# Transposing W_spatial as pairs of bf16 values in fp32 words

## The chip, the cores and the metric

The kernel runs on one core of one Trainium2 chip. The metric is the device time of one execution in microseconds, as the median of several runs; the kernel before was run three times: 140.18, 140.47 and 141.69 us. A core has five engines that run side by side, each with its own queue of instructions: TensorE (PE in the profile, with PEld for its weight loads), VectorE (DVE), ScalarE (ACT), GpSimd (POOL) and SyncE (SP, which here only issues transfers). PE writes its results to PSUM, eight banks of 512 fp32 words on each of 128 partitions. DVE and ACT copy from there to SBUF.

## What is computed

Two layers follow each other. The first is a linear attention with decay (4 batches, 8 heads, 768 positions, head size 64), worked out in blocks. Its output, 768 rows of 512 values for each batch, is the input x of the second, a gated MLP:

```python
h = np.maximum(x @ w_in, 0.0)
u, v = (h[..., :d_ff // 2].copy(), h[..., d_ff // 2:].copy())
mu = np.mean(v, axis=-1, keepdims=True)
var = np.mean((v - mu) ** 2, axis=-1, keepdims=True)
v_n = (v - mu) / np.sqrt(var + 1e-06)
v_s = np.einsum('ts,bsd->btd', w_spatial, v_n) + b_spatial[None, :, None]
gated = u * v_s
return (gated @ w_out).astype(np.float32)
```

`w_spatial` is 768 x 768 (t x s) in fp32. The sum over s is a matmul on PE, which sums over the partitions, so s must lie on the partitions: the kernel needs W_spatial transposed, and makes it itself.

## The kernel before

The work is cut into 12 units n of 256 positions, three for each batch (n // 3 is the batch). For each unit the kernel loads q, k and v, scales q and k by powers of the decay (QM, KM), turns them with transposes on PE (TQ, TK), forms masked scores (SC, MK), the attention output (AV) and from it x, already transposed (EX). Then come the second half of w_in (PV, EV), the statistics and the normalisation of v (BN, RA, RD, VN) and the first half of w_in (PU, EU). When the three units of a batch are done, the spatial matmuls (PW, line 567) and the output (PO, PH) of that batch follow.

The order of the whole is written out by hand: the string ORDER lists some 1,000 tokens. A token such as `EW.1.0.3.D` names a step, its numbers and, at the end, the engine (T for PE, D, A, P, S). Each engine takes its own tokens in that order, and an instruction that has to wait holds up all that stand behind it on its engine. Waits between engines follow from what each step reads and writes.

The steps that the change and the prediction speak of:

- WQ (line 270): six transfers bring the rows of W_spatial, 128 at a time, as fp32 into staging tiles.
- WC (line 273): casts one such chunk of rows to bf16 into `wsp_raw[:, a]` (128 partitions, 768 values). Chunks 0, 1, 3 and 4 are cast on POOL, 2 and 5 on ACT. On POOL the casts of 4 and 3 stand behind GN (line 532), a copy of one element that waits for VN.2.1.
- WT (line 550): transposes. `WT.k.i` takes the two column blocks 2k and 2k + 1 of the three row chunks of half i, six 128 x 128 blocks of bf16, into one bank. There are six WT (k from 0 to 2, i from 0 to 1), 36 transposes, in three places of PE's order: WT.1.0, WT.0.0 and WT.2.0 together, then WT.2.1 and WT.0.1, then WT.1.1.
- EW (line 559): copies the 768 values of a bank (in each partition) to `wt_sb[:, 2k:2k + 2, ...]`. EW.0.0, EW.2.1 and EW.0.1 run on ACT, EW.1.0, EW.2.0 and EW.1.1 on DVE, through the common helper `copy` (lines 178 and 180).
- VN (line 523): writes a normalised chunk of v. On DVE, VN.2.1 and VN.0.1 stand directly behind EW.1.0 and EW.2.0.
- PW (line 565): a spatial matmul for one half i and one block of 128 columns f: six matmuls over the chunks s from 0 to 5, with chunk s of `vn` as weights and `wt_sb[:, s]` as the moving operand. Chunk s of `wt_sb` is written by EW with k = s // 2. VN.0.1 writes chunk 1 of `vn`, VN.2.1 chunk 5.
- BB (line 291): spreads the bias over the partitions with an fp32 matmul of one row. FL (line 304): filling matmuls on ones. Both run in the first microseconds.
- VC (line 348): the cast of v to bf16; VC.0 is the first, on POOL.
- GM (line 571): the product of u with a finished PW on DVE. MK (line 397): the masking of the scores on DVE.

A bank of PSUM is named by the last number of a token. A step that writes a bank waits until the one that reads it last is done.

Of the kernel before, what the change touches and what calls it, by code (L numbers as in the profile page):

```python
# [8 lines left out]
FP32 = mybir.dt.float32  # L9
BF16 = mybir.dt.bfloat16  # L10
# [6 lines left out]
lam.A BR.A tab.0.A LK.0.S LQ.0.S LV.0.S LQ.1.S LK.1.S LK.2.S LV.1.S LQ.2.S WH.0.S posk.P idn.P msk.P one.D row.D  # L17
WH.1.S FL.1.512.1.1.T FL.1.256.0.1.T FL.1.256.3.1.T FL.1.256.3.1.T FL.1.512.3.1.T FL.1.256.1.1.T FL.1.512.6.1.T LB.6.T
FL.1.256.4.1.T FL.1.256.3.1.T BB.1.5.T BB.0.2.T LN.6.A LL.D mkc.D LX.A QM.0.0.P TQ.0.0.1.T KM.0.0.D KM.0.1.D QM.0.1.P
TK.0.0.0.T TK.0.1.4.T EK.0.0.0.D QM.1.0.D QM.1.1.D BE.1.5.A BE.0.2.A EQ.0.0.1.A EK.0.1.4.A VC.0.P SC.0.0.0.1.T  # L20
TQ.0.1.3.T EQ.0.1.3.A KP.0.6.T TQ.1.0.2.T SC.0.1.4.5.T TQ.1.1.3.T KM.1.1.P KM.1.0.P MK.0.0.0.1.D KM.2.1.P KM.2.0.P
VD.1.1.P TK.1.1.0.T EQ.1.0.2.A SX.0.A EK.1.1.0.A VD.1.0.A MK.0.1.4.5.D EQ.1.1.3.D FL.1.256.2.1.T TK.1.0.1.T
SC.1.1.2.3.T eps.D SY.0.6.D EK.1.0.1.D MK.1.1.2.3.D QM.2.1.P CW.0.P CW.1.P AV.0.0.6.1.T SC.1.0.4.5.T TK.2.1.0.T
# [62 lines left out]
def kernel(  # L86
# [12 lines left out]
    nc = tc.nc  # L99
    P = 128  # L100
    B, H, S, D = q.shape
# [9 lines left out]
    HW = S // 2  # L111
    NVH = NT // 2
# [5 lines left out]
    def sb(shape, dt, name):  # L118
        return const.tile(shape, dt, name=name)

    def many(n, shape, dt, name):
        return [const.tile(shape, dt, name=f"{name}_{i}") for i in range(n)]
# [7 lines left out]
    ident = sb([P, P], BF16, "ident")  # L130
    mfull = sb([P, 2, 2, P], BF16, "mfull")
    m01 = sb([P, 2, 2, Q64], BF16, "m01")
    posk = sb([P, NR, 2], FP32, "posk")
# [8 lines left out]
    mv = many(2, [P, NT, 2], FP32, "mv")  # L142
    rstd = many(2, [P, NT], FP32, "rstd")
    gap = sb([P, 120], FP32, "gap")
    win_sb = sb([P, NCH, DFF], BF16, "win_sb")
    wout_sb = sb([P, NCH, DM], BF16, "wout_sb")
    wsp_raw = sb([P, NT, S], BF16, "wsp_raw")
    wt_sb = sb([P, NT, S], BF16, "wt_sb")
# [24 lines left out]
    def bank(b):  # L173
        return ps[:, b]

    def copy(e, o, i):
        if e == "A":
            nc.scalar.activation(out=o, in_=i, func=AF.Copy)  # L178
        elif e == "D":
            nc.vector.tensor_copy(out=o, in_=i)  # L180
        else:
            nc.gpsimd.tensor_copy(out=o, in_=i)
# [43 lines left out]
    def c_ident(e):  # L226
        make_identity(nc, ident)

    def c_mask(e):
        nc.gpsimd.memset(mfull, 1.0)  # L230
        nc.gpsimd.affine_select(out=mfull, in_=mfull, compare_op=ALU.is_ge, fill=0.0, base=0,
                                pattern=[[-1, 2], [1, 2], [2, P]], channel_multiplier=-2)
# [32 lines left out]
    def stage(a):  # L265
        if a // 2 == 1:
            return wss[:, a % 2]
        return wst[a // 4].rearrange("p g f -> p (g f)")[:, (a % 2) * S:(a % 2 + 1) * S]
# [2 lines left out]
        nc.sync.dma_start(out=stage(a), in_=moe_w_spatial[a * P:(a + 1) * P, :])  # L271

    def w_c(e, a):
        copy(e, wsp_raw[:, a], stage(a))

    def w_out(e):
        nc.gpsimd.dma_start(out=wout_sb, in_=moe_w_out.rearrange("(t p) f -> p t f", p=P))
# [270 lines left out]
             bank(b).rearrange("p (f x) -> p f x", f=2))  # L548

    def w_t(e, k, i, b):  # L550
        for h in range(2):
            for a in range(NVH):
                nc.tensor.transpose(out=trip(b)[:, h, a], in_=wsp_raw[:, NVH * i + a, (2 * k + h) * P:(2 * k + h + 1) * P],  # L553
                                    identity=ident)

    def trip(b):
        return bank(b).bitcast(BF16)[:, 0:S].rearrange("p (h a x) -> p h a x", h=2, a=NVH)

    def e_w(e, k, i, b):
        copy(e, wt_sb[:, 2 * k:2 * k + 2, i * HW:(i + 1) * HW], trip(b).rearrange("p h a x -> p h (a x)"))  # L560

    def g_p(e, bb, f, i, b):
        copy(e, bank(b)[:, 0:HW], bsp[:, i * HW:(i + 1) * HW])
# [35 lines left out]
    def st_o(e, bb, t):  # L599
        eng = {"S": nc.sync, "A": nc.scalar}[e]  # L600
        eng.dma_start(out=out[bb, t * P:(t + 1) * P, :], in_=o_sb[(bb * NT + t) % NO])

    ops = dict(GT=after, GN=after_vn, one=c_ones, FL=f_l, FX=f_x, WP=w_p, WX=w_x, FN=f_n, lam=c_lam, posk=c_posk, tab=c_tab, row=c_row, eps=c_eps, LB=l_b, LN=l_n, LL=l_l, LX=l_x, idn=c_ident, msk=c_mask, mkc=c_mask2, WI=w_in, WS=w_sp, WO=w_out, BR=b_r, BB=b_b, BE=b_e, HL=hold, WH=w_h, CW=c_w, CX=c_x, WQ=w_q, WC=w_c,
               LK=ld_k, LQ=ld_q, LV=ld_v, KM=k_m, QM=q_m, DK=d_k, DQ=d_q, VC=v_c, VD=v_d, TK=t_k, TQ=t_q, EK=e_k, EQ=e_q,
               SC=s_c, MK=m_k, KV=k_v, SS=s_s, KP=k_p, SX=s_x, SY=s_y, SA=s_a, BQ=b_q, AV=a_v, EX=e_x, PV=p_v, EV=e_v, BN=b_n, RA=r_a, RD=r_d, RB=r_b,
               VN=v_n, PU=p_u, EU=e_u, WT=w_t, EW=e_w, PW=p_w, GP=g_p, GM=g_m, PO=p_o, EO=e_o, ST=st_o, PH=p_h, EH=e_h, SH=s_h)
    with tc.manual_schedule():
        for token in ORDER.split():
# [32 lines left out]
```

## Time and profile before

| | us |
|---|---|
| runs, median (lowest to highest) | 140.47 (140.18 to 141.69) |
| profiled execution: span of its instructions | 138.7 |
| profiled execution: its own whole time | not recorded; median less span is 1.8 |
| PE busy | 132.4 |
| DVE busy | 111.3 |
| ACT busy | 82.8 |
| POOL busy | 53.2 |
| the 36 transposes of W_spatial, first start to last start | 31.6 to 38.8 |

The span runs from the first to the last instruction of the program. Times in the profile count from its start. A row of a group has the line of the kernel, the engine, the operation, what it writes and reads, how many, then the busy time in us and the mean of one in ns, then the idle time of the engine just before them and what ended it. A row of a timeline has the start and the length in us, the engine, line and operation, and in brackets the idle time before. A row of the chain that ended last has start, length, engine, what is written, line and count: it is the sequence of work that led to the last instruction, followed backwards, each piece either released by the one ahead of it or standing behind it on the same engine. A matmul's own duration (219 ns for a transpose) is longer than the step from one to the next, since matmuls overlap; on the chain the step counts. Weight loads overlap with matmuls too.

### The profile page before, as it was taken

Reading aid. Unit: us, or ns where it says so; the run is one execution under the profiler, and the core shown is the slowest. Engines: PE = TensorE matmul, PEld = TensorE weight load, DVE = VectorE, ACT = ScalarE, POOL = GpSimd, SP = SyncE. Lnnn points to the kernel's source line nnn. Section 1 sums busy time; section 2 is a strip of 40 time slices with the busy share of each in tenths; the row PEclk is TensorE's granted clock in tenths of the full one; section 3 lists DMA queues with packets and bytes.
Section 4 is the critical chain, followed back from the end, with each engine's and each line's share of the span. In section 5 each row is a group of like instructions: output and inputs, shape, how many; then the busy total and the mean of one; then the engine's idle time right before and its main releaser. Section 6 shows DMA issues by size and latency. Waiting matters only on the chain.

```text
span 138.7 us, 4697 instructions
## 1 busy us (share of the span) xinstructions
PE 132.4 (95%) x1980; PEld 85.1 (61%) x1980; DVE 111.3 (80%) x229; ACT 82.8 (60%) x159; POOL 53.2 (38%) x64
## 2 busy tenths in 40 slices
PE   5998799999999999999999999999999999999990
PEld 2556665688667557667566565766655664766550
DVE  1549999989688879999979987887969988887540
ACT  3355579799846655598903678795716553961241
POOL 5178734862979676900068033209500000000000
PEclk9999999999999999999999999999999999999999
DMA  3999999999999999669796799999976594000165
GB/s 78 347 346 347 388 361 359 411 378 356 262 368 335 261 285 337 149 164 354 226 219 145 189 344 277 247 223 349 127 227 65 198 395 181 9 0 0 76 255 199
DMA packets 56873, 34.12 MB, mean 246 GB/s; under 512 B 13843, under 2 KB 52243, under 8 KB 56852
## 3 DMA queue, kind: packets, MB, share of 16 engines
q1 hardware_dynamic: 56704, 33.69, 83.7%
q8 instruction: 15, 0.25, 0.7%
q10 hardware_dynamic: 148, 0.13, 0.3%
q14 instruction: 6, 0.05, 0.1%
HBM read 24.38 MB, written 6.29 MB: 221 GB/s over the span
## 4 chain that ended last, share of the span: by engine, by line
PE 89%; DVE 5%; ACT 2%; issue 2%; DVEq 0%
PE ps L567 23%; PE ps L541 15%; PE ps L578 14%; PE ps L490 12%; PE ps L363 5%; PE ps L393 5%; PE ps L465 4%; DVE a_sb L398 3%; PE ps L456 2%; PE ps L422 2%; PE ps L306 2%; PE ps L292 2%; PE ps L553 1%; PE ps L587 1%; ACT vh L495 1%
## 5 line engine op out<-in xcount | busy, mean ns | idle before, releaser
L567 PE MATMUL ps<-wt_sb,vn 128*128 128x384 bf16 x192 | 32.4, 326 | 0.0
L328 POOL TENSOR_TENSOR kc<-k_in,lv 128x512 bf16<-128x512 f32 x20 | 20.5, 1043 | 30.7 <-DMA k_in<-in_k_dram 15.6
L398 DVE TENSOR_TENSOR a_sb<-ps,m 128x1024 bf16<-128x1024 f32 x24 | 28.7, 1218 | 2.4 <-PE ps L393 1.6
L567 PEld LDWEIGHTS <-vn 128*128 128x128 bf16 x192 | 18.5, 98 | 12.0
L541 PE MATMUL ps<-xT,win_sb 128*128 128x256 bf16 x192 | 23.8, 273 | 0.0
L490 PE MATMUL ps<-win_sb,xT 128*128 128x512 bf16 x96 | 22.7, 379 | 0.0
L578 PE MATMUL ps<-wout_sb,gT 128*128 128x512 bf16 x88 | 21.5, 380 | 0.0
L541 PEld LDWEIGHTS <-win_sb 128*128 128x128 bf16 x192 | 18.3, 98 | 4.5
L573 DVE TENSOR_TENSOR gT<-ps,uT 128x384 bf16<-128x384 f32 x32 | 17.0, 552 | 5.1 <-PE ps L567 5.1
L328 POOL TENSOR_TENSOR qc<-q_in,lqn 128x512 bf16<-128x512 f32 x17 | 17.7, 1059 | 5.0 <-DMA q_in<-in_q_dram 5.0
L505 DVE BATCH_NORM_STATS2 st<-vh 128x6 f32<-128x512 bf16 x24 | 16.3, 678 | 0.9 <-ACT vh L495 0.5
L490 PEld LDWEIGHTS <-xT 128*128 128x128 bf16 x96 | 9.0, 98 | 10.1 <-ACT xT L178 1.0
L178 ACT ACTIVATE xT<-ps 128x512 bf16<-128x512 f32 x21 | 11.5, 593 | 6.0 <-PE ps L465 6.0
L178 ACT ACTIVATE o_sb<-ps 128x512 f32<-128x512 f32 (+1 forms) x17 | 9.4, 555 | 9.3 <-PE ps L578 5.5
L495 ACT ACTIVATE vh<-ps 128x512 bf16<-128x512 f32 x19 | 10.8, 596 | 7.0 <-PE ps L490 6.9
L495 ACT ACTIVATE uT<-ps 128x512 bf16<-128x512 f32 x22 | 12.7, 594 | 3.1 <-PE ps L541 2.8
L178 ACT ACTIVATE ps<-bsp 128x384 f32<-128x384 f32 x22 | 10.5, 496 | 6.4 <-DVE gT L573 3.6
L578 PEld LDWEIGHTS <-gT 128*128 128x128 bf16 x88 | 8.1, 97 | 8.0 <-issue 0.2
L393 PE MATMUL ps<-qT,kT 64*64 64x128 bf16 x384 | 9.9, 226 | 0.6 <-DVE qT L180 0.5
L465 PE MATMUL ps<-a_sb,vb 64*64 64x128 bf16 x384 | 10.2, 217 | 0.2
L180 DVE COPY o_sb<-ps 128x512 f32<-128x512 f32 (+1 forms) x9 | 5.9, 657 | 3.3 <-PE ps L578 3.2
L465 PEld LDWEIGHTS <-vb 64*64 64x64 bf16 x384 | 7.3, 107 | 1.6 <-issue 1.5
(75 smaller groups left out, 164.5 us busy)
## 6 DMA issues: line engine op xcount, KB each, us to landing
k_in<-in_k_dram SPq DMA_DIRECT2D x12, 512.0 KB, 6.5
q_in<-in_q_dram SPq DMA_DIRECT2D x12, 512.0 KB, 6.4
v_in<-in_v_dram SPq DMA_DIRECT2D x12, 512.0 KB, 6.3
out_dram<-o_sb SPq DMA_DIRECT2D x22, 256.0 KB, 2.4
wst<-in_moe_w_in_dram SPq DMA_DIRECT2D x4, 512.0 KB, 7.7
wst<-in_moe_w_spatial_dram SPq DMA_DIRECT2D x4, 384.0 KB, 6.4
wst<-in_moe_w_out_dram SPq DMA_DIRECT2D x1, 1024.0 KB, 7.7
wss<-in_moe_w_spatial_dram SPq DMA_DIRECT2D x2, 384.0 KB, 6.7
```

The costliest lines, as they stand in the source:

```text
L178: nc.scalar.activation(out=o, in_=i, func=AF.Copy)
L328: vec(e).tensor_tensor(out=dst[n % NCA][:, u].rearrange("p u m o d -> p o (u m) d"), in0=src[n % NIN].rearrange("p (o u) m d -> p o u m d" ...
L393: nc.tensor.matmul(out=pa[o][row(c), w, j], lhsT=kT[n % NTR][row(o), u, j, c * Q64:(c + 1) * Q64], rhs=qv(n, o, u, c), start=(w == 0 and j ...
L398: nc.vector.tensor_tensor(out=a_sb[n % NA][:, i].rearrange("p o w j x -> p o w (j x)"), in0=ps[:, b0:b1 + 1:b1 - b0].rearrange("p o (w y) ...
L465: nc.tensor.matmul(out=po[c ^ o][row(w), c, i], lhsT=vb[n % NCA][row(c), 4 * o + u, j, :], rhs=a[row(c), i, o, w, j, :], start=(r == 0 and ...
L490: nc.tensor.matmul(out=bank(b), lhsT=x[:, slot(c, g)], rhs=win_sb[:, g, DH:DFF], start=(g == 0), stop=(g == NCH - 1))
L495: nc.scalar.activation(out=o, in_=i, func=AF.Relu)
L505: nc.vector.bn_stats(out=st6[p2][:, t], in_=vh[p2][:, t])
L541: nc.tensor.matmul(out=pu[:, f2].rearrange("p (c x) -> p c x", c=2), lhsT=win_sb[:, g, f * P:(f + 1) * P], rhs=x[:, slot(0, g):slot(1, g) ...
L567: nc.tensor.matmul(out=bank(b)[:, 0:HW], lhsT=vn[bb % 2][:, s, f * P:(f + 1) * P], rhs=wt_sb[:, s, i * HW:(i + 1) * HW], start=False, stop ...
L573: nc.vector.tensor_tensor(out=gT[bb % 2][:, f, cols], in0=bank(b)[:, 0:HW], in1=uT[bb % 2][:, f, cols], op=ALU.mult)
L578: nc.tensor.matmul(out=bank(b), lhsT=gT[bb % 2][:, f, t * P:(t + 1) * P], rhs=wout_sb[:, f, :], start=(f == 0), stop=(f == NCH - 1))
```

## The change

The cast WC now writes its 768 bf16 values in another order: of the column blocks 2k and 2k + 1, column x of the first and column x of the second become neighbours and so one 4-byte word. WT then reads `wsp_raw` as fp32, 384 words to a row, and transposes 128 x 128 blocks of words against an identity in fp32: three in place of six for each WT, 18 in place of 36 in all. After it a bank holds the words, each with a value of block 2k and one of block 2k + 1, and EW takes them apart when it copies: it reads the 2-byte values at a step of two, first all of one half, then all of the other. The result in `wt_sb` is as before. The fp32 identity is a new tile, filled by one copy on POOL (`idf`), placed in the order behind VC.0. Nothing else of the order changes.

```diff
-... VC.0.P SC.0.0.0.1.T
+... VC.0.P idf.P SC.0.0.0.1.T
...
+    ident4 = sb([P, P], FP32, "ident4")
...
+    def c_ident4(e):
+        nc.gpsimd.tensor_copy(out=ident4, in_=ident)
...
     def w_c(e, a):
-        copy(e, wsp_raw[:, a], stage(a))
+        copy(e, wsp_raw[:, a].rearrange("p (k x h) -> p k h x", h=2, x=P),
+             stage(a).rearrange("p (k h x) -> p k h x", h=2, x=P))
...
     def w_t(e, k, i, b):
-        for h in range(2):
-            for a in range(NVH):
-                nc.tensor.transpose(out=trip(b)[:, h, a], in_=wsp_raw[:, NVH * i + a, (2 * k + h) * P:(2 * k + h + 1) * P],
-                                    identity=ident)
-
-    def trip(b):
-        return bank(b).bitcast(BF16)[:, 0:S].rearrange("p (h a x) -> p h a x", h=2, a=NVH)
+        for a in range(NVH):
+            nc.tensor.transpose(out=bank(b)[:, a * P:(a + 1) * P],
+                                in_=wsp_raw[:, NVH * i + a].bitcast(FP32)[:, k * P:(k + 1) * P], identity=ident4)
 
     def e_w(e, k, i, b):
-        copy(e, wt_sb[:, 2 * k:2 * k + 2, i * HW:(i + 1) * HW], trip(b).rearrange("p h a x -> p h (a x)"))
+        copy(e, wt_sb[:, 2 * k:2 * k + 2, i * HW:(i + 1) * HW],
+             bank(b).bitcast(BF16)[:, 0:S].rearrange("p (y h) -> p h y", h=2))
```

More of the change, by code (lines that the diff above doesn't have):

```diff
@@ L19 @@
 FL.1.256.4.1.T FL.1.256.3.1.T BB.1.5.T BB.0.2.T LN.6.A LL.D mkc.D LX.A QM.0.0.P TQ.0.0.1.T KM.0.0.D KM.0.1.D QM.0.1.P
-TK.0.0.0.T TK.0.1.4.T EK.0.0.0.D QM.1.0.D QM.1.1.D BE.1.5.A BE.0.2.A EQ.0.0.1.A EK.0.1.4.A VC.0.P SC.0.0.0.1.T
+TK.0.0.0.T TK.0.1.4.T EK.0.0.0.D QM.1.0.D QM.1.1.D BE.1.5.A BE.0.2.A EQ.0.0.1.A EK.0.1.4.A VC.0.P idf.P SC.0.0.0.1.T
 TQ.0.1.3.T EQ.0.1.3.A KP.0.6.T TQ.1.0.2.T SC.0.1.4.5.T TQ.1.1.3.T KM.1.1.P KM.1.0.P MK.0.0.0.1.D KM.2.1.P KM.2.0.P
@@ L601, in st_o @@
         eng.dma_start(out=out[bb, t * P:(t + 1) * P, :], in_=o_sb[(bb * NT + t) % NO])
-    ops = dict(GT=after, GN=after_vn, one=c_ones, FL=f_l, FX=f_x, WP=w_p, WX=w_x, FN=f_n, lam=c_lam, posk=c_posk, tab=c_tab, row=c_row, eps=c_eps, LB=l_b, LN=l_n, LL=l_l, LX=l_x, idn=c_ident, msk=c_mask, mkc=c_mask2, WI=w_in, WS=w_sp, WO=w_out, BR=b_r, BB=b_b, BE=b_e, HL=hold, WH=w_h, CW=c_w, CX=c_x, WQ=w_q, WC=w_c,
+    ops = dict(GT=after, GN=after_vn, one=c_ones, FL=f_l, FX=f_x, WP=w_p, WX=w_x, FN=f_n, lam=c_lam, posk=c_posk, tab=c_tab, row=c_row, eps=c_eps, LB=l_b, LN=l_n, LL=l_l, LX=l_x, idn=c_ident, idf=c_ident4, msk=c_mask, mkc=c_mask2, WI=w_in, WS=w_sp, WO=w_out, BR=b_r, BB=b_b, BE=b_e, HL=hold, WH=w_h, CW=c_w, CX=c_x, WQ=w_q, WC=w_c,
                LK=ld_k, LQ=ld_q, LV=ld_v, KM=k_m, QM=q_m, DK=d_k, DQ=d_q, VC=v_c, VD=v_d, TK=t_k, TQ=t_q, EK=e_k, EQ=e_q,
```

## The prediction

> **What bounds the kernel now.** I read the page first, then the chain that ended last in order of time, then the groups by line and shape, then the timelines of single engines around the transposes. The page says which engine sets the end:
>
> ```profile
> span 138.7 us, 4697 instructions
> PE 132.4 (95%) x1980; PEld 85.1 (61%) x1980; DVE 111.3 (80%) x229; ACT 82.8 (60%) x159; POOL 53.2 (38%) x64
> PE 89%; DVE 5%; ACT 2%; issue 2%; DVEq 0%
> ```
>
> TensorE (PE) is busy 95% of the span and holds 89% of the chain, so time added to or taken from PE in the middle moves the end about one for one. The three runs have a median of 140.47 us; the span is 138.7, so 1.8 us lie around it, and I leave these as they are. A measurement of this kernel can tell about 1% (1.4 us) from no change.
>
> All the changed transposes (line 553) lie on the chain:
>
> ```profile
> 31.79 1.00 PE ps L553 x18
> 32.79 0.87 PE ps L541 x8
> 33.66 0.35 PE ps L393 x16
> 34.01 2.06 PE ps L567 x12
> 36.07 0.67 PE ps L553 x12
> 36.74 1.95 PE ps L567 x12
> 38.69 0.34 PE ps L553 x6
> 39.02 0.38 PE ps L422 x32
> 39.40 0.23 PE ps L393 x16
> 39.62 2.06 PE ps L567 x12
> 41.68 0.89 PE ps L363 x16
> ```
>
> The reader is to see three bursts, 18 + 12 + 6, in 1.00 + 0.67 + 0.34 = 2.01 us, 56 ns each, with no wait of PE between them. Call the three places A, B and C. Half of 2.01 us, 1.0, is the most that 18 fewer transposes at the same pace can bring.
>
> **Part 1, the transposes.** 36 leave, 18 come, each still 128 columns, but of 4-byte elements. No fp32 transpose is in the trace. The lower bound is the row of the same operation, 56 ns. The upper bound is the only fp32 matmul on PE, the spreading of the bias:
>
> ```profile
> 1.52 2.31 PE L306 MATMUL ps<-ones 128*128 128x512 bf16 x7 [1.52 <-DVE ones L302]
> 4.83 2.92 PE L292 MATMUL ps<-bsp,one_row 1*128 1x384 f32 x4
> L292 PEld LDWEIGHTS ps<-bsp,one_row x4: 283/332/332, 4.8 to 6.3; 1*128 1x128 f32 x4
> L306 PEld LDWEIGHTS <-ones x10: 98/133/151, 1.5 to 12.7; 128*128 128x128 bf16 x10
> ```
>
> Both stand in the slow first microseconds, so I use their ratio alone. The seven fillers (three of 512 columns, four of 256) stream 2560 columns in 2.31 us, 0.90 ns a column. The two fp32 matmuls became four instructions, 2.92 us for 2 x 384 columns, 3.8 ns a column: 4.2 times as much. Carried over, an fp32 transpose would take 4.2 x 56 = 235 ns. Between the two lies a case where only the weight load doubles (283 to 332 against up to 151 ns in the same microseconds) and sets the pace: 2 x 56 = 112 ns. I take 56 ns, because the transpose of line 553 is the nearest row in operation, shape and place, and the fp32 row multiplies and is split in two instructions. All three prices go on into the range.
>
> The Trainium skill ("TensorE: Matmul & The Clock Gate", Terms) says that on trn2 the matmul and the weight load have a transpose mode that is four times as fast for FP32. By that rule 235 would become 59 ns and the sum below would stay; by the fp32 row alone it would be that of the first rival. No run here shows which.
>
> **Part 2, the copies out of PSUM (EW).** Three run on VectorE (DVE), three on ScalarE (ACT). They now read bf16 values two apart, one from each 4-byte word.
>
> ```profile
> L180 DVE COPY wt_sb<-ps 128x768 bf16<-128x768 bf16 x3 | 1.7, 554 | 0.2
> L180 DVE CAST xT<-ps 128x512 bf16<-128x512 f32 x3 | 2.0, 665 | 0.0
> L180 DVE COPY kT<-ps 128x512 bf16<-128x512 bf16 x3 | 1.2, 416 | 2.0 <-PE ps L363 2.0
> L178 ACT ACTIVATE wt_sb<-ps 128x768 bf16<-128x768 bf16 x3 | 2.3, 809 | 0.8 <-PE ps L553 0.8
> L178 ACT ACTIVATE xT<-ps 128x512 bf16<-128x512 f32 x21 | 11.5, 593 | 6.0 <-PE ps L465 6.0
> L178 ACT ACTIVATE qT<-ps 128x512 bf16<-128x512 bf16 x4 | 2.4, 597 | 1.3 <-PE ps L363 1.2
> ```
>
> On ACT, 512 elements cost 593 ns from 4-byte words and 597 from packed ones: the new read costs it nothing, 809 stays. On DVE they cost 665 from words and 416 packed, 249 more. A strided bf16 read is not in the trace: its bounds are 554 (packed pace) and 554 + 249 x 768/512 = 928 ns (a word for each element). I take 928, as each element now sits in a word of its own, like the fp32 row's. The Trainium skill ("VectorE: DVE Perf Modes", Mode 2×_1P) asks for a step of one for the two-a-cycle mode; by it the copy is 928 and not 554, the side against this change. No run here shows a step of two.
>
> What the 0.37 us more meets at A:
>
> ```profile
> 31.40 0.72 DVE L529 TENSOR_SCALAR vn<-vh,mv,rstd 128x512 bf16<-128x512 bf16 x2
> 32.16 1.23 DVE L180 COPY wt_sb<-ps 128x768 bf16<-128x768 bf16 x2
> 33.30 0.73 DVE L529 TENSOR_SCALAR vn<-vh,mv,rstd 128x512 bf16<-128x512 bf16 x2
> 34.06 1.22 DVE L398 TENSOR_TENSOR a_sb<-ps,m 128x1024 bf16<-128x1024 f32 x1
> 33.94 0.10 PEld L567 LDWEIGHTS <-vn 128*128 128x128 bf16 x1
> 34.09 0.29 PEld L567 LDWEIGHTS <-vn 128*128 128x128 bf16 x3
> ```
>
> DVE is full here. EW.1.0 and EW.2.0 end at 33.39, then VN.2.1 and VN.0.1 end at 34.03, and the second weight load of the first spatial matmul (line 567, chunk s = 1, which is VN.0.1's output) starts at 34.09, 0.06 later. So DVE and PE arrive there together. With the change DVE is free for EW.1.0 at 32.16 as before (its transposes are done), two copies of 0.93 overlapping by 0.08 end at 33.94, the two VN 0.64 later at 34.58, and the load starts at 34.64: **+0.55 us**. PE itself would be there at 33.59, half a microsecond early, and waits about 1.05 us. The 0.50 us that A's nine fewer transposes save is therefore lost, and 0.55 more.
>
> At B the copies are ACT's. PE saves 6 x 56 = **-0.33 us**. What B waits for is the last casts of W_spatial on GpSimd (POOL), behind a marker copy that waits for VN.2.1:
>
> ```profile
> 33.77 0.30 POOL L533 CAST seen<-vn 1x1 f32<-1x1 bf16 x1 [3.45 <-DVE vn L529]
> 34.02 0.82 POOL L182 CAST wsp_raw<-wst 128x768 bf16<-128x768 f32 x1
> 34.79 0.82 POOL L182 CAST wsp_raw<-wss 128x768 bf16<-128x768 f32 x1
> 38.56 2.03 POOL L328 TENSOR_TENSOR kc<-k_in,lv 128x512 bf16<-128x512 f32 x2
> ```
>
> These move with VN by 0.55 and end at 36.16, PE arrives at 36.62: still 0.46 of cover. The four tensor products behind them (up to 40.59) feed transposes of line 363 that start at 41.68 on the chain, over 1 us later, and PE moves too.
>
> At C the copy EW.1.1 is DVE's again:
>
> ```profile
> 38.73 0.56 DVE L573 TENSOR_TENSOR gT<-ps,uT 128x384 bf16<-128x384 f32 x1 [0.35 <-PE ps L567]
> 39.20 0.55 DVE L180 COPY wt_sb<-ps 128x768 bf16<-128x768 bf16 x1
> ```
>
> It starts when the product before it is done and would end at 39.20 + 0.93 = 40.13. The third matmul of the chain's row at 39.62 (chunk s = 2, 0.17 us each) reads it at 39.96. With 0.06 for the hand-over it waits until 40.19: **+0.23 us**; the 0.17 that three fewer transposes save is lost there too.
>
> **Part 3, the casts into pairs (WC) and the fp32 identity.** Four casts on POOL and two on ACT now write every second 2-byte slot. No strided write of one element is in the trace; the packed cast's 0.82 us is the lower bound and twice it (one slot at a time where two were packed) the upper. I take 0.82: it is 1.07 ns an element, and DVE's word-at-a-time row is no faster (665 ns for 512), so nothing says that POOL packs. The new copy of the identity is 128 elements on POOL after VC.0:
>
> ```profile
> 8.61 1.03 POOL L182 CAST vb<-v_in 128x1024 bf16<-128x1024 f32 x1
> 10.88 4.04 POOL L328 TENSOR_TENSOR kc<-k_in,lv 128x512 bf16<-128x512 f32 x4 [1.24 <-DMA k_in<-in_k_dram]
> ```
>
> By the POOL cast above it is at most 0.82 us and falls into 1.24 us of waiting for a load: nothing. Without that cover it would delay the products of the second block by its length.
>
> **Sum.** A +0.55, B -0.33, C +0.23: +0.45 us, 140.47 + 0.45 = 140.9 us. At 112 ns a transpose A and C stay as they are (DVE sets both) and B saves nothing: +0.78, 141.25. I let no later part of the chain take the delay back, since DVE's longest wait is one for PE, which moves with it:
>
> ```profile
> L573 DVE TENSOR_TENSOR gT<-ps,uT 128x384 bf16<-128x384 f32 x32 | 17.0, 552 | 5.1 <-PE ps L567 5.1
> ```
>
> **Rivals.**
>
> *Slower: fp32 transposes at 235 ns.* At A the third ends at 31.79 + 0.71 = 32.50 and the ninth at 33.91; EW.2.0 then runs 33.95 to 34.88, VN.0.1 ends at 35.52, the load starts at 35.58, +1.49. B costs 6 x 235 - 670 = +0.74. At C three end at 39.40, EW.1.1 at 40.37, the reader starts at 40.43, +0.47. Sum +2.7: 143.2 us. For it: the only fp32 row on PE. Against: that row is arithmetic, in two instructions. It decides from about 150 ns on, where the total passes +1.4. Chance 0.18.
>
> *Faster: DVE reads at the packed pace.* EW.1.0 and EW.2.0 no longer wait for the ninth pair of transposes (0.11 us) and overlap (0.08): A -0.20; B -0.33; C, where EW.1.1 still ends at 39.75, -0.15. Sum -0.68: 139.8 us. For it: the values are still 2 bytes. Against: 665 against 416 ns. Chance 0.10.
>
> *POOL's casts take twice as long.* Behind VN.2.1 (33.71 + 0.55) and the marker the two last casts would end at 37.80, PE arrives at 36.62: 1.2 us of wait at B, 142.1 us. Against: 1.07 ns an element leaves no packing to lose. Chance 0.10.
>
> **How the numbers follow.** The forecast with transposes of 56 to 112 ns and DVE's copies at 0.93 has chance 0.57 and its own range 140.5 to 141.6; 0.05 is for what I don't see. The range, 139.7 to 143.1, takes in the faster rival, POOL's, and the larger part of the way to the slow transposes. Slower by over 1% (above 141.9): 0.18, most of POOL's 0.10, and a little, 0.28. Faster by over 1% would need more than the whole 1.0 us: 0.03. Within 1%: 0.69.
>
> **What would show it.** Right: 18 instructions in place of 36 at the transposes' line, 56 ns apart on the chain; DVE's copies into wt_sb at about 0.93 us and ACT's at 0.81; a new idle time of about 1 us of PE before line 567's weight load, ended by DVE's vn, and one of about 0.4 us ended by wt_sb; POOL's casts at 0.82. Wrong: two instructions for a transpose or a pitch above 150 ns; DVE's copies near 0.55; PE waiting at B for wsp_raw; or the delay gone again by the second group of spatial matmuls at 66 us.

## The result and the profile after

The changed kernel takes 142.49 us in the median (142.11 to 142.51 in four runs), the kernel before 140.33 in the runs beside it: ratio 1.0138, 95% interval 1.009 to 1.0186 (with four runs on each side this is not quite the ratio of the two medians, 1.0154). That is 2.2 us slower in the medians; the forecast was +0.45 us with a range of 139.7 to 143.1. The profiled execution took 142.5 us, its span is 140.8 us, 2.1 us longer than before. (The order has some 710 tokens, not some 1,000 as said above.)

The page of the changed kernel, first the span, then busy time of each engine, then the shares of the chain:

```profile
span 140.8 us, 4663 instructions
PE 134.0 (95%) x1962; PEld 86.0 (61%) x1962; DVE 112.8 (80%) x229; ACT 83.0 (59%) x159; POOL 54.7 (39%) x65
PE 89%; DVE 6%; issue 2%; ACT 0%; DVEq 0%
```

PE still sets the end, with 18 matmul instructions fewer. Its chain through the three places (start, length, engine, what is written, line, count; the transposes are now line 557, the spatial matmuls 569, DVE's copies 181) and, further on, at 86 us:

```profile
31.80 0.34 PE ps L557 x3
...
32.16 1.83 DVE wt_sb L181 x2
...
34.04 0.41 PE ps L398 x14
34.45 2.20 PE ps L569 x12
36.65 0.03 issue
36.67 0.88 PE ps L557 x6
37.55 1.96 PE ps L569 x12
...
39.53 0.35 DVE gT L575
...
40.01 0.96 DVE wt_sb L181
...
41.01 1.79 PE ps L569 x10
42.80 0.89 PE ps L368 x16
...
85.66 0.25 PE ps L427 x31
85.91 0.98 issue
86.89 0.21 PE ps L427
```

Two things are to be seen. DVE's copies now stand on the chain at A (32.16) and at C (40.01), where PE had run through. And the transposes of line 368 begin at 42.80 in place of 41.68, only 1.12 us later: the other 0.95 us comes at 85.91, where PE stands still for 0.98 us ahead of the last of 32 like matmuls, and the profile names no wait for it.

The groups by line and shape give the prices:

```profile
L181 DVE COPY wt_sb<-ps 128x768 bf16<-128x768 bf16 x3 | 2.8, 951 | 0.0
L557 PE MATMUL ps<-ident,wsp_raw 128*128 128x128 f32 x18 | 2.5, 276 | 0.0
L179 ACT ACTIVATE wt_sb<-ps 128x768 bf16<-128x768 bf16 x3 | 2.3, 809 | 1.4 <-DVE gT L575 1.1 <-PE ps L557 0.3
L183 POOL CAST wsp_raw<-wst 128x768 bf16<-128x768 f32 x3 | 3.1, 1045 | 0.5 <-DMA wst<-in_moe_w_spatial_dram 0.4
L179 ACT ACTIVATE wsp_raw<-wss 128x768 bf16<-128x768 f32 x1 | 1.1, 1072 | 0.0
L231 POOL CAST ident<-ident 128x128 f32<-128x128 bf16 x1 | 0.8, 753 | 0.0
```

DVE's copy went from 554 to 951 ns, ACT's stayed at 809, as forecast. The casts did not stay: on POOL three of the four have a mean of 1045 ns in place of 831, and the last two, in front of B, take 1040 and 1041 in place of 817 and 818; on ACT it is 1072 in place of 850. The transposes in C are three in 0.33 us (starts at 39.33, 39.44 and 39.55), 109 ns each, twice the bf16 pitch.

To compare executions, which differ by up to 0.5 us ahead of 31 us, I measure stretches of PE: A from the start of the first transpose of W_spatial to that of the 12th spatial matmul, B on to the 24th, C on to the 36th, D from the 96th to the 97th (73.7 to 94.7 us before). In us, against the kernel before:

| kernel | A | B | C | D |
|---|---|---|---|---|
| before (length) | 4.12 | 2.62 | 2.99 | 20.98 |
| changed | +0.57 | +0.23 | +0.31 | +0.94 |
| strided copies alone | +0.58 | 0.00 | +0.31 | 0.00 |
| changed, packed copies | -0.02 | +0.21 | -0.01 | +0.61 |
| changed, plain casts | +0.57 | -0.02 | +0.31 | +0.92 |
| fp32 transposes alone | -0.02 | -0.02 | -0.01 | +0.31 |
| changed, 72 more instructions | +0.57 | +0.23 | +0.30 | 0.00 |
| before with a delay of 1.08 us | 0.00 | +1.08 | 0.00 | +0.01 |
| fp32 transposes alone, same count | -0.01 | +0.01 | -0.01 | +0.41 |
| changed, same count | +0.58 | +0.24 | +0.31 | +0.37 |
| changed, groups of transposes behind all work | +0.57 | +0.23 | +0.31 | +0.68 |

0.57 + 0.23 + 0.31 + 0.94 = 2.05 us is the whole of the longer span. All other stretches of the changed kernel agree with before within 0.01 us. Each row is one execution. The +0.41 and +0.37 in D of the two kernels with the same count are not the stop at 86 us but waits for a transfer (experiments 7 and 8).

### The profile page after: what moved, and what is told of

It reads as the page before. It is cut to its first block, busy times and chain, and to the rows that moved or that the text cites. A ratio compares the mean times of both kernels' runs of the same rounds, so it can differ in the third digit from the quotient of the medians.

```text
span 140.8 us, 4663 instructions
## 1 busy us (share of the span) xinstructions
PE 134.0 (95%) x1962; PEld 86.0 (61%) x1962; DVE 112.8 (80%) x229; ACT 83.0 (59%) x159; POOL 54.7 (39%) x65
## 4 chain that ended last, share of the span: by engine, by line
PE 89%; DVE 6%; issue 2%; ACT 0%; DVEq 0%
PE ps L569 22%; PE ps L580 14%; PE ps L546 14%; PE ps L495 14%; PE ps L398 5%; PE ps L368 4%; PE ps L470 4%; PE ps L461 3%; PE ps L427 2%; PE ps L311 2%; PE ps L297 2%; DVE a_sb L403 2%; DVE wt_sb L181 2%; PE ps L589 1%; PE ps L557 1%
## 5 line engine op out<-in xcount | busy, mean ns | idle before, releaser
L333 POOL TENSOR_TENSOR kc<-k_in,lv 128x512 bf16<-128x512 f32 x20 | 20.5, 1040 | 30.8 <-PE ps L569 11.4
L398 PE MATMUL ps<-qT,kT 64*64 64x128 bf16 x384 | 10.7, 234 | 0.4 <-DVE wt_sb L181 0.2
L398 PEld LDWEIGHTS <-kT 64*64 64x64 bf16 x384 | 7.5, 115 | 2.2 <-issue 1.4
```

Source lines behind the costliest of these rows:

```text
L333: vec(e).tensor_tensor(out=dst[n % NCA][:, u].rearrange("p u m o d -> p o (u m) d"), in0=src[n % NIN].rearrange("p (o u) m d -> p o u m d" ...
L398: nc.tensor.matmul(out=pa[o][row(c), w, j], lhsT=kT[n % NTR][row(o), u, j, c * Q64:(c + 1) * Q64], rhs=qv(n, o, u, c), start=(w == 0 and j ...
```

## Experiments

**1. DVE's strided copies alone.** The kernel before, with the reads of the change:

```diff
-        copy(e, wt_sb[...], trip(b).rearrange("p h a x -> p h (a x)"))
+        copy(e, wt_sb[...], bank(b).bitcast(BF16)[:, 0:S].rearrange("p (y h) -> p h y", h=2))
```

> The kernel before with one part of the change alone: the copies out of PSUM read 2-byte values at a step of two (so the values in wt_sb change places; casts and transposes are those of before). Theory: the delay of the changed kernel up to 50 us is made by DVE's copies at 0.95 us in place of 0.55. Then PE's second spatial matmul comes 0.55 to 0.6 us later, the third place costs 0.25 to 0.3 us, nothing in the second: +0.85 us, 141.2 us, ratio 1.006. Rival one, the delay comes from the casts or the fp32 transposes: within 0.2 us of before. Rival two, for the other 0.95 us of the changed kernel, PE's idle time at 86 us: it follows from any delay of PE of about 1 us against the transfers: then the sum here is +1.8 us, 142.1 us. The theory has it from the place of a 256-instruction boundary of PE's stream, which here is that of before: no idle time over 0.3 us between 80 and 90 us.

141.31 us against 140.43, ratio 1.0063 (1.0044 to 1.0082). Its chain (spatial matmuls here line 568, transposes 553):

```profile
31.80 0.35 PE ps L553 x6
32.17 1.83 DVE wt_sb L180 x2
34.01 0.04 issue
34.05 0.41 PE ps L393 x14
34.46 2.20 PE ps L568 x12
36.66 0.67 PE ps L553 x12
37.33 1.96 PE ps L568 x12
...
39.79 0.96 DVE wt_sb L180
```

The same detours over DVE as in the changed kernel, with bf16 transposes, and B at its old length (0.67 + 1.96). A and C are DVE's copies and nothing else. Between 80 and 90 us PE does not wait, though it comes 0.9 us late: rival two falls for this delay.

**2. Packed copies in the changed kernel.**

```diff
-             bank(b).bitcast(BF16)[:, 0:S].rearrange("p (y h) -> p h y", h=2))
+             bank(b).bitcast(BF16)[:, 0:S].rearrange("p (h y) -> p h y", h=2))
```

> The changed kernel with packed reads in the copies out of PSUM (so pairs stay together and wt_sb holds other values); casts into pairs and 18 fp32 transposes stay. Theory: DVE's copies are back at 0.55 us, the first and third place cost nothing, the second up to 0.1 us, because GpSimd's casts of 1.04 us then end at about 36.1 us, where PE arrives: up to 50 us it is within 0.2 us of before. Whether the idle time at 86 us stays isn't decided by the copies: 140.5 us without it, 141.5 with it. Rival, casts or transposes make the delay: +0.8 us or more up to 50 us.

141.23 us against 140.43, ratio 1.0051 (1.0028 to 1.0073). A and C are back, B stays at +0.21, twice what I allowed, and 0.65 us of waiting at 84.7 us stays. The copies decide A and C, not B and not D.

**3. Plain casts in the changed kernel.**

```diff
-        copy(e, wsp_raw[:, a].rearrange("p (k x h) -> p k h x", h=2, x=P),
-             stage(a).rearrange("p (k h x) -> p k h x", h=2, x=P))
+        copy(e, wsp_raw[:, a], stage(a))
```

> The changed kernel with casts in the plain order of before (so other values are transposed); fp32 transposes and strided copies stay. Theory: casts take 0.82 us again on GpSimd and 0.85 on ScalarE in place of 1.04 and 1.07, and the second place loses the wait for the last cast, 0.2 to 0.25 us; the first and third stay at 0.55 and 0.3. Up to 50 us +0.85 us over before in place of +1.1. Total 142.2 with the idle time at 86 us, 141.2 without. Rival, the second place is slow because of the fp32 transposes themselves: it stays at +1.1 us up to 50 us.

141.86 us against 140.43, ratio 1.0103 (1.0075 to 1.0131). B is back to -0.02: all of B was the casts'. Their timeline in the changed kernel on POOL, and then the weight loads of the transposes behind them:

```profile
34.37 0.30 POOL L538 CAST seen<-vn 1x1 f32<-1x1 bf16 x1 [3.74 <-DVE vn L534]
34.61 1.04 POOL L183 CAST wsp_raw<-wst 128x768 bf16<-128x768 f32 x1
35.58 1.04 POOL L183 CAST wsp_raw<-wss 128x768 bf16<-128x768 f32 x1
```

```profile
36.67 0.31 PEld L557 LDWEIGHTS ps<-ident,wsp_raw 128*128 128x128 f32 x3 [0.41 <-POOL wsp_raw L183]
```

The second cast ends at 36.62, just when PE is done with the spatial matmuls at 36.65. In the kernel before, the first weight load of the burst was pulled ahead to 35.74, while matmuls still ran:

```profile
35.74 0.10 PEld L553 LDWEIGHTS <-wsp_raw 128*128 128x128 bf16 x1
```

Now it comes at 36.67, and load and matmul start from nothing. With packed copies the casts ended earlier, but PE came earlier by as much, which is why B stayed in experiment 2.

**4. The fp32 transposes alone**, plain casts and packed copies (both edits above in the changed kernel).

> The 18 fp32 transposes alone, with the fp32 identity: casts in the plain order and packed reads in the copies (so wt_sb holds other values). Theory: 18 at 109 ns take the time of 36 at 56 ns, so up to 50 us it is within 0.1 us of before: no gain and no loss. For the rest: if the idle time at 86 us follows from the 36 PE instructions fewer alone, 141.3 us; if it needs the delay, 140.3. Rival, an fp32 transpose has a cost besides its pitch (a slow switch between types, a late weight load): +0.5 us or more by 50 us.

140.96 us against 140.43, ratio 1.0034 (1.0014 to 1.0054). Its three bursts on the chain (line 556):

```profile
31.50 0.98 PE ps L556 x9
...
35.76 0.65 PE ps L556 x6
...
38.37 0.33 PE ps L556 x3
```

1.96 us, against 2.01 for the 36 of bf16: nothing is gained where the gain was meant to be, and nothing lost. The +0.53 us of the median is not there but in D, where PE waits again:

```profile
84.05 0.42 PE L426 MATMUL ps<-vb,kc 64*64 64x64 bf16 x31
84.81 0.21 PE L426 MATMUL ps<-vb,kc 64*64 64x64 bf16 x1 [0.34 <-issue]
```

**5. Where D comes from.** In the changed kernel and in experiments 2 to 4 PE stops ahead of the 32nd of the 32 matmuls of this step (line 427 or 426, the state update of unit 7). Counting PE's recorded instructions (weight loads, matmuls and the few semaphore and drain instructions of its sequencer, and a matmul for each weight load where its record is missing), the weight load behind the stop is number 2754 in the changed kernel and in experiments 2 to 4. The kernel before has such a stop of 0.44 us at number 450 and one of 0.10 at 706, 256 further; 2754 is nine times 256 on from 450. A transfer queue of kind "instruction" brings pieces of 16,384 bytes; the row of the page of before is

```profile
q8 instruction: 15, 0.25, 0.7%
```

and 15 pieces of 256 are 3,840 of PE's 3,960 loads and matmuls. The changed kernel with 288 more at its end (experiment 9) has one piece more:

```profile
q8 instruction: 16, 0.26, 0.7%
```

So I took the stop for a wait for the next 256 instructions. All kernels that stop there have 36 instructions fewer ahead of this place, which moves the boundary by 36. It lies in the same step either way: in the kernel before number 2754 is the weight load of the 14th of the 32 matmuls, at 84.44 us, and PE does not stop:

```profile
84.38 0.42 PE L422 MATMUL ps<-vb,kc 64*64 64x64 bf16 x32
```

The pieces themselves tell more. In the five profiles with the stop (the changed kernel and experiments 2, 3, 4 and 9) number 2754 starts 2.2 to 2.3 us after the piece's packet began to move, whenever that was; in the six without it the packet began 2.4 us or more ahead. From number 2498, 256 before, to 2754 PE needs 4.4 us in the kernel before and in the changed kernel alike, the stop left out. What differs is the packet, which began 2.0 us after number 2498 before, 1.5 to 1.8 in experiments 1 and 6 to 8, and 2.6 to 3.3 in the five.

The first test was 72 more instructions in the changed kernel, by halving matmuls:

```diff
+            for y in ((slice(0, 256), slice(256, 512)) if n < 3 else (slice(0, 512),)):
+                nc.tensor.matmul(out=bank(b)[:, y], lhsT=x[:, slot(c, g)], rhs=win_sb[:, g, DH:DFF][:, y], ...)
...
+            for y in ((slice(0, 256), slice(256, 512)) if bb == 0 and t < 3 else (slice(0, 512),)):
```

> The changed kernel with 36 matmuls of 512 columns (line 495, units 0 to 2, and line 580, three row chunks of the first batch) split in two halves of 256 columns, the same work in 72 more PE instructions. Theory: the 0.98 us of idle time of PE at 86 us is a wait for the next 256 instructions, which are fetched over the busy transfer queues; 72 more instructions ahead move the boundary from the short matmuls of line 427 into the long ones of line 495 before them and ask for the fetch earlier. The splits cost about 36 x 3 ns = 0.1 us. So 142.5 - 0.95 + 0.1 = 141.6 us, and no idle time of PE over 0.3 us between 80 and 90 us. Rival, PE waits there for data or a buffer: the idle time stays at about 1 us in line 427, 142.6 us.

141.91 us against 140.42, ratio 1.0107 (1.0076 to 1.0139). D is +0.00: the stop at 86 us is gone. The boundary did not come to lie where the expectation has it, in the long matmuls of line 495, but in the short ones of line 470 behind them (number 2754 at 85.62 us), and its packet had begun at 78.84, 6.8 us ahead. The total came down by 0.6 us, not 0.85. In its profile the stops at the two early boundaries are longer, 0.78 us at 16.4 and 0.41 at 23.3; but the first lies ahead of all that was added, and goes from 0.22 to 0.78 us over the profiles of all these kernels, so that one is spread between executions. Where the rest of the 0.25 us went is not shown.

**6. A delay alone.**

```diff
-WT.0.1.0.T
+WT.0.1.0.T FL.5.512.4.1.T
```

> The kernel before with five filling matmuls of 512 columns (1.08 us, 10 PE instructions more) behind the transposes of the second place, into a bank that is free there; nothing else changes. Theory: PE sets the end, so the delay reaches the end in full, +1.1 us, 141.4 us; the boundary of 256 instructions lies 10 instructions earlier than before, so no idle time at 86 us. Rival one, a delay of 1.1 us by itself meets the transfers and brings the idle time: +2.0 us, 142.3 us. Rival two, later slack takes a delay of PE back: under +0.5 us.

141.61 us against 140.42, ratio 1.0088 (1.0061 to 1.0115): +1.19 us for 1.08 us of fillers. PE's time does reach the end in full, and no stop comes at 86 us. Yet the profiled execution, the slowest of six (142.44, the others 141.34 to 141.73), has one elsewhere, at number 1474 (450 + 4 x 256):

```profile
46.59 0.39 PE L393 MATMUL ps<-qT,kT 64*64 64x128 bf16 x14
47.69 0.24 PE L393 MATMUL ps<-qT,kT 64*64 64x128 bf16 x2 [0.71 <-issue]
```

Its packet had begun at 45.50, 2.2 us ahead, as at the other stops. So rival one has a part of the truth: shifting PE against the transfers can bring such a stop too, at another boundary and not in every execution.

**7 and 8. The same number of instructions.** 18 of the first batch's spatial matmuls are halved, so that from 39 us on PE's stream has the count of before; once with the fp32 transposes alone, once with the whole change.

```diff
+            for y in ((slice(0, 192), slice(192, HW)) if bb == 0 and i == 0 and f < 3 else (slice(0, HW),)):
+                nc.tensor.matmul(out=bank(b)[:, y], lhsT=..., rhs=wt_sb[:, s, i * HW:(i + 1) * HW][:, y], ...)
```

> The 18 fp32 transposes alone, as in the run of that kind, and 18 of the first batch's spatial matmuls (384 columns) split in halves of 192, so that from 38 us on PE's stream has as many instructions as before. Theory: the +0.53 us that the fp32 transposes alone cost is the wait for instructions at 84.5 us (0.34 us in its profile, from execution to execution somewhat more), and not the transposes. It goes away, the splits cost 18 x 3 ns: 140.4 to 140.6 us, ratio 1.000 to 1.001, no idle time of PE over 0.1 us between 80 and 90 us. Rival, the wait there has to do with the transposes or with the data: idle time and +0.5 us stay.

140.65 us against 140.40, ratio 1.0016 (1.0002 to 1.003), a little above the 1.000 to 1.001 expected; of the +0.53 us about half is left, and the interval overlaps with that of experiment 4. In the profile PE has no stop between 80 and 90 us.

> The changed kernel whole, with the same 18 splits. Theory: the +0.57, +0.23 and +0.31 us of the three places stay, the 0.94 us of waiting for instructions at 86 us goes: 140.4 + 1.1 + 0.05 = 141.6 us, ratio 1.008, no idle time of PE over 0.1 us between 80 and 90 us. Rival, the wait follows from PE's delay against the transfers: 142.5 us.

141.56 us against 140.40, ratio 1.0082 (1.0066 to 1.0099). The place of the stop, first in the changed kernel, then in this one:

```profile
85.49 0.42 PE L427 MATMUL ps<-vb,kc 64*64 64x64 bf16 x31
86.89 0.21 PE L427 MATMUL ps<-vb,kc 64*64 64x64 bf16 x1 [0.98 <-issue]
```

```profile
85.26 0.42 PE L427 MATMUL ps<-vb,kc 64*64 64x64 bf16 x32
```

All 32 go through, with A, B and C together at +1.13 us in this profile (12.58 to 13.71 from the first transpose to the 48th whole spatial matmul). The stop at 86 us belongs to the 36 instructions and not to the delay: PE comes there later than the kernel before in experiments 1, 6 and 8, and does not stop; in experiment 4 it runs 0.3 us ahead of the kernel before, and stops. D is not back to the length of before, though. In the seventh run PE waits 0.28 us at 74.9 us for a transfer that turns k, and is 0.4 us late from there on:

```profile
PE ps L397 <- DMA kT<-kc: 0.3, 1, 0.3
```

The eighth's profile has one of 0.30 of the same kind at 95 us, and is 0.37 us later from there on. Why these transfers came late I did not follow, so whether a same count costs nothing beyond A, B and C is not shown.

**9. The pitch by itself.** Five groups of 24 on PE behind all work of the changed kernel (its time says nothing): bf16 transposes; fp32 transposes; fp32 with 64 columns of weights; fp32 with 64 moving columns; plain fp32 matmuls.

```diff
+                nc.tensor.transpose(out=bank(SB)[:, 0:P], in_=w.bitcast(FP32)[:, ...], identity=ident4)
...
+                nc.tensor.matmul(out=bank(SB)[:, 0:P], lhsT=w.bitcast(FP32)[:, ...], rhs=ident4, ...)
```

> The changed kernel with five groups of 24 instructions on PE behind all its work, into an unused bank, with nothing to wait for: bf16 transposes 128x128; fp32 transposes 128x128; fp32 transposes with 64 columns of weights and 128 moving columns; fp32 transposes with 128 columns of weights and 64 moving columns; plain fp32 matmuls of 128 columns with the same operands. Its time is not compared. Theory: an fp32 transpose streams its moving columns at half pace, 2 x 53 ns, so the pitches are 56, 109, 109, 56 and, for the plain fp32 matmul in two passes, 4 x 53 = 215 ns or more. Rival, the fp32 weight load (140 ns against 98) sets the pitch: 56, 109, about 56, 109. By the Trainium skill (TensorE: Matmul & The Clock Gate, Terms: transpose mode four times as fast for FP32) the second would be a fourth of the fifth.

PE's timeline (start, length, count), and the weight loads of the groups:

```profile
136.97 1.50 PE L568 MATMUL ps<-ident,wsp_raw 128*128 128x128 bf16 x24
138.31 2.79 PE L570 MATMUL ps<-ident,wsp_raw 128*128 128x128 f32 x24
140.94 2.78 PE L572 MATMUL ps<-ident,wsp_raw 128*64 128x128 f32 x24
143.66 1.72 PE L574 MATMUL ps<-ident,wsp_raw 64*128 64x64 f32 x24
145.31 5.62 PE L576 MATMUL ps<-ident,wsp_raw 128*128 128x128 f32 x48
```

```profile
L572 PEld LDWEIGHTS ps<-ident,wsp_raw 128*64 128x64 f32 x24 | 2.6, 111 | 0.0
L570 PEld LDWEIGHTS ps<-ident,wsp_raw 128*128 128x128 f32 x24 | 2.6, 141 | 0.0
```

First to last start gives 56, 110, 109 and 65 ns an instruction, and 114 for the plain fp32 matmul, which is two instructions: 228 ns. Half the weights (111 in place of 141 ns a load) change nothing, half the moving columns nearly halve the pitch, while the weight load stays at 140 ns: the moving fp32 words set it, at half the pace of bf16 (110 against 56 ns). The rival falls, though at 64 moving columns something holds the pitch at 65 where 56 was expected. That group has half the rows too (64 x 64 identity), so by itself it does not part columns from rows; but the bias matmul in the prediction has a single row, and an instruction of it also takes 2.1 times as long a column as the bf16 fillers beside it.

## Why the prediction was right and wrong

The sign, the places A and C and DVE's price were right; of the 2.05 us in the profile, 0.88 are those two, where 0.78 were forecast (+0.55 measured +0.57, +0.23 measured +0.31). The measured time lies in the range, but near its upper end, and above the likeliest case's own 140.5 to 141.6; over 1% slower had a chance of 0.28. That the range holds it is in part luck: its upper end was there for transposes of 235 ns or for POOL's casts at twice their time, and neither came, while 0.94 us came from a stop that no term and no rival has.

*A, the cause.* The copies took 0.95 us against 0.93, VN.0.1 ended at 34.63 against 34.58, as worked out. But the forecast had PE at line 567 early and waiting there for about 1 us. It waits earlier and less. At 109 ns the transposes save PE nothing, and the scores ahead of line 567 (line 398, from 34.04) write banks 3 and 4, which EW.1.0 and EW.2.0 read, and so wait for the copies themselves; the second weight load then follows VN.0.1 at 34.68:

```profile
34.04 0.41 PE L398 MATMUL ps<-qT,kT 64*64 64x128 bf16 x14 [0.21 <-DVE wt_sb L181]
34.68 0.28 PEld L569 LDWEIGHTS <-vn 128*128 128x128 bf16 x3 [0.21 <-DVE vn L534]
```

I had not looked at which bank the work between the transposes and the spatial matmuls writes.

*Part 1, the price of a transpose, failed.* "I take 56 ns, because the transpose of line 553 is the nearest row" was wrong; 109 ns is the middle case, though by the moving words and not, as argued for it, by the weight load. The upper bound, 235 ns, was right for what it described (228 for a plain fp32 matmul). The Trainium skill's factor of four ("TensorE: Matmul & The Clock Gate", Terms) does not agree with the run, if these transposes run in that mode, which no row names: 228 to 110 ns is a factor of 2.1. The wrong price cost the sum only at B, 0.33 us, since DVE sets A and C. The prediction has this case too, with +0.78 us as its sum.

*Part 3, the casts, failed.* "I take 0.82" came to 1.045 us on POOL, between the bounds. Two casts in a row are 0.45 us late behind a marker that is late itself, and +0.23 us came at B where -0.33 was forecast; PE waiting there for wsp_raw is one of the prediction's own signs of being wrong. Experiment 3 shows it. The 0.46 us of cover were too many as well: they count to the chain's row at 36.07, while the first weight load of the burst stands at 35.74, so that the cover was about 0.14 us. (C has the same slip: its third spatial matmul starts at 39.89 and not at 39.96, 0.07 of the 0.08 us by which C came out longer.) The same +0.22 us on ACT (850 to 1072) hurt nobody, and the new copy of the identity, 0.75 us, cost nothing, as forecast.

*Part 2* holds in both halves: 951 ns on DVE, 809 on ACT. The rule of the Trainium skill on steps of one ("VectorE: DVE Perf Modes", Mode 2×_1P) agrees with the 951 here, and with experiment 2, where a packed read is back at 0.55 us. The rival of the packed pace falls.

*What the sum had no term for: +0.94 us.* "36 leave, 18 come" was priced as time on PE alone. It also shortens PE's stream by 36 instructions, and the boundary of a fetched piece moved from the 14th to the 32nd of the matmuls at 85 us. That the stop goes with the instruction count is shown (it takes 0.34 to 0.98 us in the five profiles of kernels with 36 fewer, and is absent in the six others, those of experiments 7 and 8 among them, which have the 36 back). That it is a wait for instructions no wait in the trace names; it follows from the spacing of 256, from the number of pieces, and from the time between a piece's packet and the end of the stop, 2.2 to 2.3 us in all five. Why the piece comes just then too late stays open: in the changed kernel its packet moved at 84.64 us, 3.3 us after the boundary before it was crossed, in the kernel before 2.0 us after. What asks for a piece stays open too, since in experiment 5 the packet moved 2.4 us ahead of that boundary. The queues are full there, which speaks for waiting behind loads; but in the kernel before they are as full from 80 to 82 us:

```profile
DMA  9999999999999999999999999999999999999999
```

This is the row of the changed kernel from 81 to 87 us in 40 slices. I did not try a kernel with fewer loads in that stretch.

"No later part of the chain takes the delay back" was right: experiment 6 passes 1.08 us on in full.

## What to carry to other kernels

Packing two values into a word moved the work here and did not halve it: count what the wider element costs on PE (here twice a bf16 column, so 18 took the time of 36), what taking the words apart costs the reader, and what putting them together costs the writer. When a copy on a full engine gets longer, list every instruction behind it, and every bank that it keeps. And when an edit changes the number of PE instructions, look for stops that the profile gives no cause for at multiples of 256, before the edit is given the blame or the credit for them.

## What the runs showed of the hardware

- An fp32 transpose of 128 columns starts every 110 ns, a bf16 one every 56, a plain fp32 matmul every 228. With 64 columns of weights it stays at 109; with 64 moving columns (and 64 rows) it is 65.
- A write of bf16 values at a step of two costs POOL and ACT the same 0.22 us on 768 elements, 0.29 ns each, while ACT's read at a step of two costs nothing (809 ns both ways).
- PE stops at numbers 450, 706, 1474 and 2754 of its recorded instructions, always a multiple of 256 apart, for 0.1 to 1.0 us, while the transfer queues are full. The first instruction behind such a boundary started no sooner than 2.2 us after the packet of its piece began, which itself takes 0.9 us.
